# A list scheduler that counts TensorE's instruction blocks, and chunk loads moved behind Gram loads

## The chip, the cores and the metric

The kernel runs on one core of a Trainium2 chip. What counts is the device time of one execution in microseconds (us), from the first to the last instruction with what lies around them; runs of the same kernel are compared by their median.

## The reference

Three layers follow each other. The first is a delta-rule attention with 4 batches, 8 heads, 768 tokens and a head dimension of 48:

```
k_n = k / (norm(k) + 1e-6)
for t in range(S):
    y[t] = q[t] @ state
    v_old = state applied to k_n[t]
    state = state + beta[t] * outer(k_n[t], v[t] - v_old)
```

Its output, 3072 tokens by 384, goes through a soft mixture of experts (logits x @ phi, a softmax over the tokens to make 32 slots, eight experts with 1024 hidden units and a ReLU, a softmax over the slots to combine), and then through a feed-forward layer with 2048 hidden units and g = h * sigmoid(1.702 h). All of it is float32.

## The kernel before

The 768 tokens are cut into 24 chunks of 32 (NS, C). All 32 heads are worked on at once. The work has a *planned* part and a *plain* part.

The planned part is the attention, the logits and the dispatch. For each chunk i there are Gram matrices: load_g brings k and q of the chunk (kq), copy_k copies k, gram runs the matmuls for K with K ("G") and for Q with K ("P") into a PSUM bank, and gram_out copies them out. Four chunks are a group. For each group, solve inverts the triangular systems on VectorE by 31 pairs of steps (lines 517 and 521), between a transpose of the Gram matrices in and one of the result out (both line 477). Chunk i then runs as a chain: V (minus v into PSUM), KS (old state times k), a copy to rbd, U (the inverse times that), a copy to ubd, S (the new state), a copy to sbd; beside it QS and Y give the output. The next chunk needs sbd. load_c brings a chunk's own data (kc, v, k, qc) to the tile cs, which has three buffers; scale_v scales v on GpSimd with the solve's norms (nr). logits transposes the output and multiplies by phi.

Every such step is a call of Plan.add with its engine, an estimated duration, the keys that it reads and writes, and, for TensorE, the columns that it streams. Nothing is sent to an engine yet. Plan.issue then makes a list schedule: listed takes, step by step, for each engine the ready operation with the best rank, and gives it a start time; issue repeats this for several weights and alternates it with backward passes, and keeps the schedule with the shortest length. The operations of each engine, SP's DMA issues among them, are sent in the order of these start times. So the estimates decide the order; on the chip, semaphores decide the times.

Plan.fill goes through the planned TensorE operations: where the gap to the next is over FILL[0] + 2 TURN = 0.54 us and fewer than NEED = 4500 columns lie in the last WIN = 3.4 us of the plan, it puts in dummy matmuls (filler, line 356), to keep TensorE at work. 18 more (PRE) stand at the start.

A float32 matmul call gives two weight loads and two matmuls on TensorE, a transpose one of each.

The plain part follows: the experts and the feed-forward layer, in the order in which they are written down. The diff doesn't touch it.

Before the change the loads of chunks 0 and 1 are added to the plan with i = 0 and i = 1, without a dependency:

```python
        if i < VB - 1:
            load_c(i)
```

Of the kernel before, what the change touches and what calls it, by code (L numbers as in the profile page):

```python
# [19 lines left out]
B, H, S, D = 4, 8, 768, 48  # L20
C = 32
NS = S // C
GS = 4
# [5 lines left out]
VB, UB, XB, XTB, LB = 3, 2, 5, 4, 1  # L29
# [4 lines left out]
NA, NBS = 4, 4  # L34
# [23 lines left out]
class Plan:  # L58
# [10 lines left out]
    WAITS = (4.0, 8.0, 20.0)  # L69
    ROUNDS = 24  # L70

    WIN, NEED = 3.4, 4500
    FILL = (0.24, 384)

    def __init__(self, tc, filler=None):
        self.tc = tc
        self.filler = filler
        self.ops = []
        self.names = []
        self.kinds = []  # L80
        self.wr, self.rd, self.first = {}, {}, {}
        self.beside = {}

    def add(self, eng, dur, fn, reads=(), writes=(), after=0.0, nm="", cols=0, deps=(), beside=None):
        self.names.append(nm)
        k = len(self.ops)
        if eng == "pe":
            dur *= self.PACE
        self.kinds.append(self.KINDS.get(nm.split(".")[0], "rows") if eng == "pe" else eng)
        deps = set(deps)  # L90
        for r in reads:
            if r in self.wr:
                deps.add(self.wr[r])
            self.rd.setdefault(r, []).append(k)
        for w in writes:
            if w in self.wr:
                deps.add(self.wr[w])
            deps.update(self.rd.get(w, ()))
        for w in writes:
            self.wr[w] = k  # L100
            self.rd[w] = []
        deps.discard(k)
        if beside is not None:
            self.beside[k] = beside
            deps.add(beside)
        self.ops.append((eng, dur, fn, deps, after, cols))
        return k
# [7 lines left out]
    def issue(self):  # L115
        ops = self.ops
        n = len(ops)
        pred = [[(d, self.lat(d, k)) for d in ops[k][3]] for k in range(n)]
        succ = [[] for _ in range(n)]
        for k in range(n):  # L120
            for d, l in pred[k]:
                succ[d].append((k, l))
        tail = [0.0] * n
        for k in range(n - 1, -1, -1):
            tail[k] = ops[k][1] + max([tail[q] + l for q, l in succ[k]], default=0.0)
        best = None
        for w in self.WAITS:
            rank = [-t for t in tail]
            for _ in range(self.ROUNDS):
                start = self.listed(rank, pred, succ, w)  # L130
                if best is None or self.length(start) < best[0] - 1e-6:
                    best = (self.length(start), start)
                back = self.listed([-(start[k] + ops[k][1]) for k in range(n)], succ, pred, w)
                end = max(back[k] + ops[k][1] for k in range(n))
                rank = [end - back[k] - ops[k][1] for k in range(n)]
        self.makespan, start = best
        order = sorted((round(start[k], 6), k, k) for k in range(n))
        self.order = order
        idle = self.fill(order) if self.filler else {}
        self.fillers = sum(idle.values())  # L140
        for _, _, k in order:
            for _ in range(idle.get(k, 0)):
                self.filler(self.names[k])
            ops[k][2]()
# [1 line left out]
    def length(self, start):  # L146
        return max(start[k] + o[1] for k, o in enumerate(self.ops) if o[0] not in ("sp", "aq") and o[0][0] != "v")

    def listed(self, rank, pred, succ, wait):


        ops, kinds = self.ops, self.kinds
        n = len(ops)
        left, ready, start = [len(p) for p in pred], [0.0] * n, [0.0] * n
        free, cand, best, last = {}, {}, {}, None
        for k in range(n):
            free.setdefault(ops[k][0], 0.0)
            cand.setdefault(ops[k][0], set())
            if not left[k]:
                cand[ops[k][0]].add(k)  # L160
        stale = set(cand)
        for _ in range(n):
            for e in stale:
                best[e] = None
                for k in cand[e]:
                    t = max(free[e] + (self.TURN if e == "pe" and last not in (None, kinds[k]) else 0.0), ready[k])
                    b = (rank[k] + wait * t, t, k)
                    if best[e] is None or b < best[e]:
                        best[e] = b
            stale.clear()  # L170
            t, e, k = min((b[1], e, b[2]) for e, b in best.items() if b)
            cand[e].discard(k)
            start[k] = t
            t += ops[k][1]
            free[e] = t
            stale.add(e)
            if e == "pe":
                last = kinds[k]
            if e == "pool" and k not in self.beside:
                free["dve"] = max(free["dve"], start[k]) + self.HELD  # L180
                stale.add("dve")
            for q, l in succ[k]:
                left[q] -= 1
                ready[q] = max(ready[q], t + l)
                if not left[q]:
                    cand[ops[q][0]].add(q)
                    stale.add(ops[q][0])
        return start
# [34 lines left out]
def delta_moe_kernel(ctx, tc, kq, vt, kt, bu, phi, w1, w2, win, wout, out):  # L223
    nc = tc.nc
    P = 128
# [84 lines left out]
    kqd = [t_[:, 0:2048].rearrange("p (z h u t) -> p z h u t", z=2, h=2, u=16) for t_ in slots[0:NA]]  # L310
# [65 lines left out]
    def cost(eng, n):  # L376
        return {"dve": (n + 62) / 960.0, "act": 0.052 + n / 1200.0, "pool": 0.15 + 0.00166 * n, "padd": 0.15 + 0.0021 * n}[eng]

    def dma(dst, src, key, d=0.73):
        pl.add("sp", d, lambda: nc.sync.dma_start(dst, src), (), key if isinstance(key, list) else [key], after=2.0)  # L380

    def load_g(i):
        a = i % NA
        for h in range(2):
            dma(kqd[a][64 * h : 64 * h + 48, :, h], kq[i, 64 * h : 64 * h + 48], [("kqd", a, h)] + [("kqd", a, h, z) for z in range(2) if i < 2 * NA], 0.75)
        if i < KCOPY:
            copy_k(i)
        else:
            dma(kds[a][0:112], kq[i, :, 0], [("kd", a, 0), ("kd", a, 1)], 0.85)
# [411 lines left out]
    for i in range(NS):  # L801
        if i == 0:
            load_first()
            for z in range(2):
                for n in range(GS):

                    gram(n, z, [pl.wr["bank", GS - 1]] if z else ())
                if z == 0:
                    pl.wr["bank", GS - 1] = len(pl.ops) - 1
                for n in range(GS):  # L810
                    gram_out(n, z)
            clear_blocks()
        elif GS <= i < 3 * GS:
            grams(i)
        if i < LEAD:
            solves(i)
        if i == 1:
            setup_loads()
        if i < VB - 1:
            load_c(i)  # L820
    clear_banks()
    for i in range(NS):
        n = i + VB - 1
# [317 lines left out]
```

## Time and profile before

| | |
|---|---|
| median of 3 runs | 513.24 us (511.08 to 516.22) |
| profiled execution | 516.4 us |
| its span, first to last instruction | 514.7 us |
| TensorE busy | 470.0 us, 91% of the span |
| VectorE busy | 310.4 us, 60% |
| ScalarE busy | 280.2 us, 54% |
| GpSimd busy | 72.9 us, 14% |
| mean granted TensorE clock, share of full speed | 0.954 |

Durations below come from the profiled execution. Its span leaves out 1.7 us around the instructions. PE is TensorE's matmul, PEld its weight load, DVE VectorE, ACT ScalarE, POOL GpSimd, SP the engine that issues DMAs.

### The profile page before, as it was taken

Reading aid. Unit: us, or ns where it says so; the run is one execution under the profiler, and the core shown is the slowest. Engines: PE = TensorE matmul, PEld = TensorE weight load, DVE = VectorE, ACT = ScalarE, POOL = GpSimd, SP = SyncE. Lnnn points to the kernel's source line nnn. Section 1 sums busy time; section 2 is a strip of 40 time slices with the busy share of each in tenths; the row PEclk is TensorE's granted clock in tenths of the full one; section 3 lists DMA queues with packets and bytes.
Section 4 is the critical chain, followed back from the end, with each engine's and each line's share of the span. In section 5 each row is a group of like instructions: output and inputs, shape, how many; then the busy total and the mean of one; then the engine's idle time right before and its main releaser. Section 6 shows DMA issues by size and latency. Waiting matters only on the chain.

```text
span 514.7 us, 17917 instructions
## 1 busy us (share of the span) xinstructions
PE 470.0 (91%) x7684; PEld 394.7 (77%) x7684; DVE 310.4 (60%) x836; ACT 280.2 (54%) x621; POOL 72.9 (14%) x113
## 2 busy tenths in 40 slices
PE   8789996888987779878999899999999999999997
PEld 8667765556764555645665799999999999999997
DVE  4969998698999999440453998332323323333322
ACT  8353574756684766555342765545454545545452
POOL 5001101021032111400411655000000000000000
PEclk9687999989998997869999999999999999999999
DMA  8787778886357897997599540100100100100101
GB/s 172 185 205 185 190 215 243 222 246 186 108 154 235 272 312 211 300 391 297 183 422 383 175 163 2 62 0 1 62 1 0 63 1 0 62 0 23 39 3 61
DMA packets 35071, 77.65 MB, mean 151 GB/s; under 512 B 4208, under 2 KB 15728, under 8 KB 33840
## 3 DMA queue, kind: packets, MB, share of 16 engines
q1 hardware_dynamic: 34992, 76.51, 47.7%
q8 instruction: 60, 0.98, 0.8%
q14 instruction: 19, 0.16, 0.1%
HBM read 71.39 MB, written 5.11 MB: 149 GB/s over the span
## 4 chain that ended last, share of the span: by engine, by line
PE 78%; issue 8%; ACT 7%; DVE 3%; DMA 3%; SPq 1%; ACTq 0%; DVEq 0%
PE ps_s L1085 13%; PE ps_y L1085 7%; PE ps_g L1085 7%; PE ps_t L1085 6%; PE ps_s L582 4%; PE ps_y L563 4%; PE ps_x L554 3%; PE ps_x L548 3%; ACT sbd L593 3%; PE ps_t L356 3%; PE ps_x L571 3%; DMA wa<-in_kq_dram 3%; PE ps_x L1044 2%; PE ps_s L952 2%; PE ps_g L445 2%
## 5 line engine op out<-in xcount | busy, mean ns | idle before, releaser
L1049 DVE TENSOR_TENSOR glo<-wa,ghi 128x512 fp32r<-128x512 f32 x96 | 71.4, 744 | 127.1 <-ACT wa L1048 127.0
L1085 PE MATMUL ps_s<-wo,ghi 128*128 128x384 f32 x300 | 81.2, 335 | 0.0
L1047 ACT ACTIVATE ghi<-ps_x 128x512 fp32r<-128x512 f32 x64 | 38.4, 600 | 64.5 <-PE ps_x L1044 63.7
L521 DVE TENSOR_TENSOR wb<-wb,wb 128x87 f32<-128x87 f32 (+23 forms) x211 | 67.6, 338 | 1.2
L517 DVE TENSOR_TENSOR wb<-wb,wb 128x87 f32<-128x87 f32 (+24 forms) x211 | 63.4, 317 | 1.3
L593 ACT COPY sbd<-ps_s 64x384 f32<-64x384 f32 x92 | 43.6, 474 | 24.5 <-PE ps_s L582 19.3
L1085 PEld LDWEIGHTS ps_s<-wo,ghi 128*128 128x128 f32 x300 | 54.8, 188 | 1.9
L1085 PE MATMUL ps_g<-wo,ghi 128*128 128x384 f32 x150 | 50.3, 335 | 0.0
L1085 PE MATMUL ps_y<-wo,ghi 128*128 128x384 f32 x150 | 50.3, 335 | 0.0
L700 POOL TENSOR_TENSOR cs<-cs,nr 128x384 f32<-128x384 f32 x24 | 21.8, 916 | 134.3 <-DVE nr L509 39.4
L1085 PE MATMUL ps_s<-wo,glo 128*128 128x384 f32 x150 | 40.6, 335 | 0.0
L1085 PE MATMUL ps_t<-wo,ghi 128*128 128x384 f32 x120 | 40.2, 335 | 0.0
L1048 ACT ACTIVATE wa<-ps_x 128x512 f32<-128x512 f32 x64 | 38.0, 594 | 0.0
L1047 ACT ACTIVATE ghi<-ps_y 128x512 fp32r<-128x512 f32 x32 | 19.2, 600 | 33.0 <-PE ps_y L1044 32.7
L554 PE MATMUL ps_x<-sbd,cs 112*32 112x96 f32 x736 | 27.8, 270 | 10.1 <-issue 7.2
L558 ACT COPY rbd<-ps_x 128x384 f32<-128x384 f32 x48 | 23.0, 488 | 22.9 <-PE ps_x L554 17.3
L554 PEld LDWEIGHTS ps_x<-sbd,cs 112*32 112x32 f32 x736 | 18.1, 119 | 17.3 <-issue 9.9
L356 PE MATMUL ps_t<-warm 128*128 128x96 f32 x142 | 28.0, 342 | 1.1 <-DVE zeros L317 1.1
L575 ACT COPY ubd<-ps_x 128x384 f32<-128x384 f32 x48 | 20.9, 483 | 14.8 <-PE ps_x L571 14.7
L1085 PEld LDWEIGHTS ps_y<-wo,ghi 128*128 128x128 f32 x150 | 28.1, 188 | 0.8
L1085 PEld LDWEIGHTS ps_g<-wo,ghi 128*128 128x128 f32 x150 | 28.2, 188 | 0.7
L563 PE MATMUL ps_y<-sbd,cs 112*32 112x96 f32 x736 | 26.0, 273 | 2.8 <-ACT x L603 1.5
(289 smaller groups left out, 970.0 us busy)
## 6 DMA issues: line engine op xcount, KB each, us to landing
cs<-in_kq_dram SPq DMA_DIRECT2D x48, 224.0 KB, 4.3
wa<-in_kq_dram SPq DMA_DIRECT2D x42, 192.0 KB, 4.3
wb<-in_w_dram SPq DMA_DIRECT2D x16, 384.0 KB, 6.9
wb<-in_w_dram SPq DMA_DIRECT2D x4, 1536.0 KB, 13.4
cs<-in_vt_dram SPq DMA_DIRECT2D x24, 192.0 KB, 3.9
wa<-in_w_dram SPq DMA_DIRECT2D x3, 1536.0 KB, 10.6
out_dram<-wa SPq DMA_DIRECT2D x24, 192.0 KB, 1.9
cs<-in_kt_dram SPq DMA_DIRECT2D x23, 192.0 KB, 3.6
```

What stands on the lines that cost most here:

```text
L356: nc.tensor.matmul(ps[bank][:, 416:512], warm, warm[:, 0:96], start=True, stop=True)
L517: engs[e].tensor_tensor(tmp, xx[:, lo:top, j : j + 1].to_broadcast([P, n, m]), gu[:, j : j + 1, j + 1 :].to_broadcast([P, n, m]), op=ALU.mult)
L521: engs[e].tensor_tensor(xx[:, lo:top, j + 1 :], xx[:, lo:top, j + 1 :], tmp, op=ALU.add)
L554: nc.tensor.matmul(px[g][32 * j : 32 * j + 32, c % 2, :, j % 2], kci[0:112, 4 * j + c], sbd[0:112, j, c].rearrange("p h e -> p (h e)"), st ...
L558: pl.add(re_[g], cost(re_[g], 384), lambda g=g: copy[re_[g]](rbd[:, 2 * g : 2 * g + 2].rearrange("p c h q e -> p (c h q e)"), ps[f"x{g}"][ ...
L563: nc.tensor.matmul(py[c // 2][32 * j : 32 * j + 32, c % 2].rearrange("p h e -> p (h e)"), qci[0:112, 4 * j + c], sbd[0:112, j, c].rearrang ...
L593: apart(sbs, e, copy[e](sbn[r, :, 2 * z : 2 * z + 2, h], ps_s[z][r]))
L700: t = nc.gpsimd.tensor_tensor(v_, v_, nr[:, 8 * st : 8 * st + 8].unsqueeze(2).to_broadcast([P, 8, D]), op=ALU.mult)
L1047: nc.scalar.activation(ghis[k % 3], phs[k % 3], AF.Gelu_apprx_sigmoid)
L1048: nc.scalar.activation(ggs[k % 3], phs[k % 3], AF.Gelu_apprx_sigmoid)
L1049: nc.vector.tensor_tensor(glos[k % 3], ggs[k % 3], ghis[k % 3], op=ALU.subtract)
L1085: nc.tensor.matmul(po[f][:, 0:DM], l_[:, 128 * f : 128 * f + 128], w_out(fc, r), start=(fc == 0 and l_ is ghi and r == 0), stop=False)
```

## The change

The planner gets a table of how many matmul calls an operation has (CALLS), and in its forward passes a count: when 64 (BLOCK) calls are full, the next block starts at the earliest 4.0 us (FETCH) after the block before, and TensorE's free time moves on accordingly. The count begins at 34 (AHEAD). Backward passes don't count. The operation's start time stays; its end moves. The loads of chunks 0 and 1 are added with chunk 7 and depend, in the plan, on the last Gram load of that chunk. Both stand on the same queue, so no semaphore comes with it.

```diff
+    CALLS = {"V0": 4, "V1": 4, "KS0": 4, "KS1": 4, "QS0": 4, "QS1": 4, "U0": 16, "S0": 8, "S1": 8, "Y": 16, "G": 4, "P": 3.5, "T": 1, "L": 8, "D": 4}
+    FETCH, BLOCK, AHEAD = 4.0, 64, 34
...
+        self.calls.append(self.CALLS.get(nm.split(".")[0], 1) + (1 if cols == 664 else 0))
...
-                start = self.listed(rank, pred, succ, w)
+                start = self.listed(rank, pred, succ, w, True)
...
-    def listed(self, rank, pred, succ, wait):
+    def listed(self, rank, pred, succ, wait, forward=False):
...
+        calls, block = self.AHEAD, 0.0
...
+            if e == "pe":
+                last = kinds[k]
+                calls += self.calls[k]
+                if forward and calls >= self.BLOCK:
+                    calls -= self.BLOCK
+                    part = ops[k][1] * min(1.0, calls / max(self.calls[k], 1))
+                    at = max(t - part, block + self.FETCH)
+                    t, block = at + part, at
             free[e] = t
             stale.add(e)
-            if e == "pe":
-                last = kinds[k]
...
+    ahead = []
+
     def dma(dst, src, key, d=0.73):
-        pl.add("sp", d, lambda: nc.sync.dma_start(dst, src), (), key if isinstance(key, list) else [key], after=2.0)
+        return pl.add("sp", d, lambda: nc.sync.dma_start(dst, src), (), key if isinstance(key, list) else [key], after=2.0, deps=list(ahead))
...
-            dma(kqd[a][64 * h : 64 * h + 48, :, h], kq[i, 64 * h : 64 * h + 48], [("kqd", a, h)] + [("kqd", a, h, z) for z in range(2) if i < 2 * NA], 0.75)
+            pl.first["kq", i] = dma(kqd[a][64 * h : 64 * h + 48, :, h], kq[i, 64 * h : 64 * h + 48], [("kqd", a, h)] + [("kqd", a, h, z) for z in range(2) if i < 2 * NA], 0.75)
...
-        if i < VB - 1:
-            load_c(i)
+        if i == 2 * GS - 1:
+            ahead.append(pl.first["kq", i])
+            for n in range(VB - 1):
+                load_c(n)
+            ahead.clear()
```

## Rows read from the trace of the kernel before

**Rows 1.** Busy time by stretch: us, busy (instructions) by engine, granted clock, DMA share, GB/s.

```profile
55.00:157.00 102.00, 86.51 (x3035) 64.20 (x3027) 92.11 (x296) 69.81 (x176) 16.40 (x20) 0.97 0.70 199
157.00:245.00 88.00, 70.57 (x2012) 47.45 (x2012) 60.66 (x178) 52.02 (x134) 14.04 (x35) 0.86 0.85 285
245.00:515.00 270.00, 263.44 (x1789) 242.56 (x1779) 114.51 (x180) 131.50 (x259) 32.84 (x31) 1.00 0.21 81
```

**Rows 2.** The page: TensorE's busy time and instructions; instruction queue: packets, MB, share.

```profile
PE 470.0 (91%) x7684; PEld 394.7 (77%) x7684; DVE 310.4 (60%) x836; ACT 280.2 (54%) x621; POOL 72.9 (14%) x113
...
q8 instruction: 60, 0.98, 0.8%
```

**Rows 3.** Busy time by stretch, between long issue waits, and one dense stretch.

```profile
80.00:89.33 9.33, 7.20 (x254) 5.47 (x254) 7.81 (x24) 5.94 (x14) 0.62 (x2) 1.00 0.82 253
...
159.30:175.57 16.27, 12.52 (x381) 8.32 (x381) 16.27 (x63) 9.86 (x27) 2.81 (x3) 0.90 0.75 233
...
131.00:147.50 16.50, 15.60 (x553) 11.20 (x537) 16.17 (x62) 12.33 (x33) 2.49 (x3) 1.00 0.43 134
```

**Rows 4.** TensorE's waits, 55 to 245 us: us, times, longest (first, last of seven).

```profile
PE ps_x L554 <- issue: 7.2, 5, 2.0
...
PE ps_x L548 <- issue: 0.4, 1, 0.4
```

**Rows 5.** Timeline of TensorE; in brackets, idle before and its releaser.

```profile
108.52 0.38 PE L445 MATMUL ps_g<-wa 112*32 112x64 f32 x10 [2.54 <-issue]
```

**Rows 6.** Timeline of VectorE: transposes of the solves.

```profile
33.08 1.97 DVE L477 STREAM_TRANSPOSE wb<-gs 128x1024 f32<-128x1024 f32 x1 [4.08 <-ACT gs L463]
...
50.27 2.00 DVE L477 STREAM_TRANSPOSE gs<-wb 128x1024 f32<-128x1024 f32 x1
57.98 2.00 DVE L477 STREAM_TRANSPOSE wb<-wb 128x1024 f32<-128x1024 f32 x1
...
114.02 2.18 DVE L477 STREAM_TRANSPOSE wb<-wb 128x1024 f32<-128x1024 f32 x1
...
204.10 2.00 DVE L477 STREAM_TRANSPOSE gs<-wb 128x1024 f32<-128x1024 f32 x1
```

**Rows 7.** Timeline of TensorE: first Gram parts, fillers, V and U of some chunks.

```profile
13.20 0.65 PE L445 MATMUL ps_g<-wa 112*32 112x64 f32 x32 [0.79 <-DMA wa<-in_kq_dram]
...
16.87 0.53 PE L445 MATMUL ps_x<-wa 112*32 112x64 f32 x19 [2.27 <-issue]
...
49.04 5.38 PE L356 MATMUL ps_t<-warm 128*128 128x96 f32 x46
54.35 0.86 PE L548 MATMUL ps_x<-cs,negi 128*32 128x192 f32 x16
...
55.53 0.89 PE L571 MATMUL ps_x<-rbd,gs 64*32 64x96 f32 x32
...
119.73 0.73 PE L571 MATMUL ps_x<-rbd,wb 64*32 64x96 f32 x26
...
216.00 0.56 PE L571 MATMUL ps_x<-rbd,gs 64*32 64x96 f32 x32
```

**Rows 8.** Timeline of SP's DMA issues at the start.

```profile
7.04 0.34 SPq L380 DMA_DIRECT2D cs<-in_kq_dram  x1
13.95 8.07 SPq L380 DMA_DIRECT2D wa<-in_kq_dram  x8
22.07 0.57 SPq L380 DMA_DIRECT2D cs<-in_kq_dram  x1
```

**Rows 9.** Busy time by stretch, where the moved loads would lie.

```profile
22.00:31.00 9.00, 9.00 (x218) 7.31 (x217) 7.01 (x35) 3.93 (x8) 0.00 (x0) 0.66 0.97 230
```

**Rows 10.** Timeline of ScalarE: the last Gram copy of the third group.

```profile
49.44 0.38 ACT L468 COPY wb<-ps_y 128x256 f32<-128x256 f32 x1
```

**Rows 11.** Fillers alone (line 356), by stretch: PE and PEld busy, clock, DMA.

```profile
55.00:157.00 102.00, 0.46 (x2) 0.30 (x2) 0.97 0.70 199
157.00:245.00 88.00, 0.46 (x2) 0.30 (x2) 0.86 0.85 285
```

More of the change, by code (lines that the diff above doesn't have):

```diff
@@ L79, in __init__ @@
         self.names = []
-        self.kinds = []
+        self.kinds, self.calls = [], []
         self.wr, self.rd, self.first = {}, {}, {}
```

## Prediction

> **What bounds the kernel now.** I read the busy time by stage first [rows 1]. The last 270 us, from 245 us on, are the experts and the second feed-forward layer; there TensorE is busy 263.4 us. The planner does not order that part, so the change can only move the 245 us ahead of it. In those, no engine is full: from 55 to 157 us TensorE is busy 86.5 of 102 us and VectorE 92.1, from 157 to 245 us TensorE 70.6 of 88 and VectorE 60.7, at a granted clock of 0.86 against 0.97 in the stretch before.
>
> Next I asked how TensorE gets its instructions. Queue 8 moved 60 packets, 0.98 MB in all, so 16 KB a packet; TensorE ran 7684 matmuls and as many weight loads [rows 2]. That is 256 instructions, or 128 matmul-and-load pairs, to a packet, which I call a block. Then I counted pairs between long waits that the profile puts down to "issue", that is to nothing it sees [rows 3]: 254 from one such wait to the second after it, 381 over a third stretch. These are 2 and 3 times 127, a block less a few semaphore instructions. So these waits fall at block borders, once a block is used up and the next is not there.
>
> The price of a border has two forms. As a rate: 131 to 147.5 us holds 553 pairs [rows 3], 4.32 blocks at 3.82 us each, with TensorE busy 15.6 of 16.5 us. All of 55 to 157 us holds 3035 pairs, 23.7 blocks at 4.30 us; 157 to 245 us holds 2012, 15.7 blocks at 5.60 us [rows 1]. The first stretch is within 13% of the quickest rate seen, the second is not near it. As waits: TensorE's list of waits has seven lines released by "issue" from 55 to 245 us, 23.5 us in all [rows 4]; one of 2.54 us stands in the middle of a Gram matrix [rows 5]. That list is the most that spacing can give back.
>
> **The change part by part.** Nothing that computes is added or removed. The planner's cost of TensorE gains a rule: 64 calls (each fp32 call is two pairs, so 64 are a block) may not start less than 4.0 us after the 64 before. The load order changes, and with both the order on every engine. I take four terms against the profiled execution, 516.4 us.
>
> (a) *The start.* VectorE runs the first triangular solve, then stops 4.08 us until 33.08 us for the second group's Gram copies [rows 6], with the rest of solve 0 queued behind that transpose. The planner thought those copies earlier. One reason it could not know is TensorE's border wait of 2.27 us before 16.87 us, in the Gram matrices that hold the buffers of the next loads [rows 7]. If the planner counts it, the transpose moves behind more of solve 0 and VectorE fills the hole. Bounds: nothing, and the whole 4.08 us. I take 2 us, by the 2.27 us row. It reaches the end only if chunk 0 follows: its first matmul stands at 54.35 us behind 46 records of fillers from 49.04 us, and its U at 55.53 us though solve 0's matrix is turned by 52.27 us [rows 6, 7]. Fillers are placed by the same plan, so I let the whole front move: -2.
>
> (b) *The loads.* Four of the eight loads of chunks 0 and 1 left SP by 7.04 us, ahead of the eight second-group Gram loads that start at 13.95 us; the others stood behind those already, from 22.07 us [rows 8]. So only four are moved, some 0.8 MB. What the Gram loads gain is small, for they wait on TensorE's reading of their buffers, not on SP; the one wait for data here is TensorE's 0.79 us before 13.20 us [rows 7]. On the other side, the 0.8 MB now lie in 22 to 31 us, where the DMA engines are 97% busy at 230 GB/s [rows 9]: 3.5 us more of queue, ahead of the third group's Gram loads. What hides it: the copies of that group end at 49.82 us [rows 10] and VectorE takes them at 57.98 us [rows 6], 8.2 us later; chunk 0's own data is not read before 47 us. On SP the four pass the eight Gram loads and nothing else; POOL's queue loses nothing, for its first scaling of v waits for the solve, not for the load. I take 0, bounds -0.8 and, if that cover is gone, +3.5.
>
> (c) *The borders.* Bound of the gain: all 23.5 us of waits; the first stretch at 3.82 us a block would be 90.6 us, so 11.4 of them could go there. Bound of the loss: a worse order can cool TensorE; if the first stretch had the clock of the second, its 86.5 us busy would become 97.6, +11. Nearer to the truth is a fraction of the gain. A border's wait goes only if TensorE would have waited for another engine at that moment, or if less urgent work stands there. VectorE stands against most of it in the first stretch: solve 2's matrix is turned at 116.2 us and chunk 8's U starts at 119.73 us, 3.5 us later [rows 6, 7], so TensorE may gain no more than that before VectorE is late. At the end there is room: the last solve is done at 206.1 us, the U that needs it starts at 216.00 us [rows 6, 7]. I take a quarter of 23.5: -6.
>
> (d) *Fillers.* These dummy matmuls go wherever the plan shows TensorE idle by over 0.54 us and few columns in the window before. The stalls that the planner now models look idle to that rule. From 55 to 245 us there are now four filler records, two fillers [rows 11]. The 46 records before chunk 0, 23 fillers, took 5.38 us [rows 7], 0.23 us each. With a filler at one border in six of the 39, 6 to 7 fillers, that is +1.5. Bounds: 0, and one or two at each border, 9 to 18 us, if none hides in the wait.
>
> Sum: -2 + 0 - 6 + 1.5 = -6.5, so 509.9 us for an execution like the profiled one. That one lies 3.2 us above the median of the runs; taken from the median 513.24, it is 506.7, and I say 507.
>
> [...] The longest border wait here is 2.54 us [rows 5]. [...]
>
> **The rivals.**
> *Rate, not waits* (0.27): between 55 and 157 us blocks and VectorE both fill the time, so an order that moves waits only moves them; what one chunk saves the next spends. For it: 4.30 against 3.82 us a block, VectorE busy 92.1 of 102. Against: 10 us slack at the last solve. Then (a) -2, (c) at most -1.5, (d) +1.5: 511 to 513, say 512.
>
> *Fillers in the modelled stalls* (0.15, the side of slower): the stall is at the border, the fillers stand after it in TensorE's stream, so the engine first waits for its block and then runs them. Two at each of 39 borders are 78, 17.9 us with 78 calls or 1.2 more blocks, 4.7 us; less (a) and (c), 8: +14, if all lie on the path, half of it if half do: 520 to 527. It decides from 35 fillers in 55 to 245 us (8 us at 0.23); above that the change loses.
>
> *The count drifts* (0.10): the plan counts no fillers of the fill rule and takes 3.5 calls for a Gram part that issues three from chunk 4 on. The 23 fillers before chunk 0 [rows 7] alone are a third of a block. Then the modelled borders lie in other instructions than the chip's, the change doesn't do what it says, and the order is just another order: 513, give or take 6.
>
> *Borders cost nothing* (0.03): the issue waits have another cause in the stream and stay whatever the spacing, so (c) is 0: 513.24 - 2 + 1.5, again 513. Against it stand the multiples of 127 [rows 3]. [...]
>
> **How the numbers follow.** My forecast, 507, has 0.45; its own range is 499 to 512: 513.2 - 4.1 - 12 + 1.5 with the whole hole and half of the waits gone, 513.2 - 3 + 1.5 with no hole filled and an eighth of them gone. The range for 8 in 10 reaches up into the rivals: 498 to 521. Within 1%, about what a measurement of this kernel can tell from no change, is 508.1 to 518.4. Faster by more: 0.38 of my case, 0.06 of rate, 0.03 of drift, 0.47 together. Slower by more: 0.13 of fillers, 0.03 of drift and 0.02 of the rest, 0.18. Same: 0.35.
>
> **What would show it.** (a): the hole before the second Gram transpose on VectorE under 2.5 us and chunk 0's first U before 54 us. (b): four more loads of chunk data behind the Gram loads on SP, and no wait for them on POOL or TensorE. (c): the issue lines of TensorE from chunk 0 on sum to under 18 us, and us per block in the later stretch falls from 5.60. (d): filler records in the chunk stage between 4 and 30. The stage from 245 us on must keep its 270 us. I'm wrong if the issue waits shrink while the waits for ScalarE's copies grow by as much, if the granted clock of the second stretch drops below 0.86, or if fillers pass 70 records.

## The result and the profile after

The change makes the kernel slower by a little. In runs side by side on one chip the kernel before took 517.19 us (median of 21, two of them far off at 711 and 1435 us) and the changed one 519.82 us (median of 21, 515.92 to 524.45); the ratio is 1.0073, 95% interval 1.0048 to 1.0097. Run again beside other kernels it gave 1.0063 (1.0036 to 1.009). In some executions a kernel takes over 1.5% longer than in its fastest; the ratios leave these out, and a * in the table of experiments stands where the profiled execution was such a one. The forecast was 507, 6.2 us below the 513.24 that it started from; the kernel before itself took 4 us more here than in its first three runs.

| profiled execution | before | after |
|---|---|---|
| time / span | 516.4 / 514.7 us | 519.82 / 518.1 us |
| mean granted clock | 0.954 | 0.957 |
| chunk 0's V starts, last Y ends | 54.35, 245.1 us | 55.55, 247.6 us |
| issue waits of TensorE between the two | 23.5 us | 27.7 us |
| from the last Y to the plain part's first matmul | 7.5 us | 8.5 us |
| plain part | 262.1 us | 262.0 us |

The last rows of the table already hold the answer in outline: the plain part is the same, and all of the 3.4 us by which the span is longer lie in the planned part. Of them, 2.5 are there when the last Y ends. The other 1.0 comes behind it: the new order leaves more of the logits work (one transpose and one product with phi more) behind the last Y. The plain part starts here, first before, then after:

```profile
252.62 1.50 PE L920 MATMUL ps_x<-wa,sit 128*32 128x256 f32 x24
256.10 1.50 PE L936 MATMUL ps_x<-wa,sit 128*32 128x256 f32 x24
```

This is the page of the changed kernel, as in [rows 2]. The work is the same: ten matmul records more, which are fillers.

```profile
PE 470.5 (91%) x7694; PEld 395.2 (76%) x7694; DVE 314.6 (61%) x836; ACT 280.3 (54%) x621; POOL 73.6 (14%) x113
...
q8 instruction: 60, 0.98, 0.8%
```

Busy time by stretch, in the columns of [rows 1] (length, then busy time and count of PE, PEld, DVE, ACT, POOL, then granted clock, DMA share, GB/s):

```profile
0.00:55.00 55.00, 48.85 (x858) 40.35 (x859) 41.31 (x184) 26.79 (x53) 9.15 (x27) 0.84 0.73 170
55.00:157.00 102.00, 86.51 (x2915) 63.35 (x2916) 91.87 (x294) 67.78 (x170) 17.51 (x19) 0.95 0.72 203
157.00:245.00 88.00, 68.02 (x2065) 46.57 (x2066) 66.96 (x180) 52.59 (x135) 14.10 (x37) 0.90 0.88 283
248.00:518.00 270.00, 264.09 (x1784) 242.86 (x1783) 114.51 (x180) 131.54 (x259) 32.82 (x31) 1.00 0.21 81
```

Between 55 and 157 us TensorE is busy for the same 86.51 us as in [rows 1], but did 120 records fewer (2915 for 3035). At 128 records a block that is 4.48 us a block, for 4.30 before. In the later stretch it is 5.45 for 5.60. So the plan did not make the early blocks quicker, and the late ones hardly.

Then TensorE's list of waits from 55 to 248 us, the lines released by "issue", for comparison with [rows 4] (us in total, times, longest):

```profile
PE ps_s L595 <- issue: 8.0, 5, 4.4
PE ps_x L567 <- issue: 5.5, 5, 2.0
PE ps_y L612 <- issue: 4.6, 4, 2.1
PE ps_y L576 <- issue: 4.1, 3, 1.7
...
PE ps_x L561 <- issue: 1.9, 1, 1.9
PE ps_x L584 <- issue: 1.4, 2, 0.7
...
PE ps_g L458 <- issue: 1.2, 1, 1.2
PE ps_t L627 <- issue: 0.6, 1, 0.6
PE ps_t L638 <- issue: 0.4, 1, 0.4
```

They add up to 27.7 us with the small ones and have moved to other lines (the largest sum was KS, line 554, before; it is S, line 595, now), but have not shrunk. The longest is 4.4 us, for 2.54 before [rows 5], and it lies on the chain from chunk to chunk. The timeline of TensorE shows it in the second half (S1) of chunk 7's state update; the first rows are the start of chunk 0:

```profile
48.90 6.71 PE L367 MATMUL ps_t<-warm 128*128 128x96 f32 x58
55.55 0.86 PE L561 MATMUL ps_x<-cs,negi 128*32 128x192 f32 x16
56.34 0.69 PE L367 MATMUL ps_t<-warm 128*128 128x96 f32 x4
56.95 0.67 PE L584 MATMUL ps_x<-rbd,gs 64*32 64x96 f32 x32
...
115.55 0.71 PE L595 MATMUL ps_s<-ubd,cs 64*48 64x96 f32 x24
120.70 0.57 PE L595 MATMUL ps_s<-ubd,cs 64*48 64x96 f32 x8 [4.44 <-issue]
...
127.82 0.56 PE L584 MATMUL ps_x<-rbd,wb 64*32 64x96 f32 x32
```

A block ends after 24 of the 32 matmuls. What follows waits for the last 8: the copy to sbd, then KS, and so chunk 8's U at 127.82 us, 16.0 us after chunk 7's at 111.83. Before, these two U were 7.2 us apart, and the widest gap between any two was 11.1. The busy time of the two stretches from that wait on shows what came with it:

```profile
115.90:120.70 4.80, 0.36 (x20) 0.22 (x9) 4.11 (x12) 0.35 (x2) 0.00 (x0) 0.92 0.50 111
120.70:127.80 7.10, 7.10 (x179) 6.01 (x178) 0.00 (x0) 4.46 (x12) 1.56 (x2) 0.57 0.48 146
```

TensorE hardly works for 4.8 us, and then runs at a granted clock of 0.57, with 179 records in 7.1 us. The clock was 1.00 from 115.9 to 119.9 us, 0.50 from 121 to 126 and 1.00 again from 126.9 us on. VectorE does nothing in the second of the two.

At the start the timeline above has 62 records of fillers around chunk 0's V (58 and 4) where before had 48, 46 of them in [rows 7]; chunk 0's U is at 56.95 us, 1.4 later than before in this execution. VectorE's hole before the second Gram transpose, 4.08 us in [rows 6], is now 5.78:

```profile
35.05 1.96 DVE L490 STREAM_TRANSPOSE wb<-gs 128x1024 f32<-128x1024 f32 x1 [5.78 <-ACT gs L476]
```

The issues of SP, against [rows 8]:

```profile
5.15 0.43 SPq L393 DMA_DIRECT2D cs<-in_vt_dram  x1
5.62 0.43 SPq L393 DMA_DIRECT2D cs<-in_kq_dram  x1
6.10 0.63 SPq L393 DMA_DIRECT2D cs<-in_kt_dram  x1
14.35 8.52 SPq L393 DMA_DIRECT2D wa<-in_kq_dram  x8
22.92 0.58 SPq L393 DMA_DIRECT2D cs<-in_vt_dram  x1
```

Three chunk loads still stand ahead of the eight Gram loads. They are chunk 2's: the third buffer of cs is free too, the change gave no dependency to its loads, and they slipped into the place that those of chunks 0 and 1 left.

### The profile page after: what moved, and what is told of

The parts are those of the page before. It is cut to its first block, busy times and chain, and to the rows that moved or that the text cites. A ratio compares the mean times of both kernels' runs of the same rounds, so it can differ in the third digit from the quotient of the medians.

```text
span 518.1 us, 17928 instructions
## 1 busy us (share of the span) xinstructions
PE 470.5 (91%) x7694; PEld 395.2 (76%) x7694; DVE 314.6 (61%) x836; ACT 280.3 (54%) x621; POOL 73.6 (14%) x113
## 4 chain that ended last, share of the span: by engine, by line
PE 76%; issue 9%; ACT 7%; DMA 4%; DVE 3%; SPq 1%; ACTq 0%; DVEq 0%
PE ps_s L1101 13%; PE ps_y L1101 6%; PE ps_g L1101 6%; PE ps_t L1101 6%; PE ps_s L595 4%; PE ps_y L576 4%; DMA wa<-in_kq_dram 4%; ACT sbd L606 3%; PE ps_x L567 3%; PE ps_x L561 3%; PE ps_t L367 3%; PE ps_x L584 3%; PE ps_x L1060 2%; PE ps_t L627 2%; PE ps_s L968 2%
## 5 line engine op out<-in xcount | busy, mean ns | idle before, releaser
L534 DVE TENSOR_TENSOR wb<-wb,wb 128x31 f32<-128x31 f32 (+25 forms) x211 | 66.5, 335 | 2.0
L530 DVE TENSOR_TENSOR wb<-wb,wb 128x135 f32<-128x135 f32 (+25 forms) x211 | 65.4, 328 | 2.0
L567 PE MATMUL ps_x<-sbd,cs 112*32 112x96 f32 x736 | 29.8, 279 | 8.1 <-issue 5.5
L1063 ACT ACTIVATE ghi<-ps_y 128x512 fp32r<-128x512 f32 x32 | 19.2, 600 | 33.0 <-PE ps_y L1060 33.0
L595 PE MATMUL ps_s<-ubd,cs 64*48 64x96 f32 x736 | 23.3, 257 | 11.4 <-issue 8.0
L571 ACT COPY rbd<-ps_x 128x384 f32<-128x384 f32 x48 | 23.2, 490 | 18.5 <-PE ps_x L567 11.5
L576 PE MATMUL ps_y<-sbd,cs 112*32 112x96 f32 x736 | 25.7, 259 | 5.5 <-issue 4.1
L595 PEld LDWEIGHTS ps_s<-ubd,cs 64*48 64x48 f32 x736 | 17.0, 122 | 17.8 <-issue 10.7
## 6 DMA issues: line engine op xcount, KB each, us to landing
wa<-in_kq_dram SPq DMA_DIRECT2D x42, 192.0 KB, 4.4
cs<-in_vt_dram SPq DMA_DIRECT2D x24, 192.0 KB, 4.4
out_dram<-wa SPq DMA_DIRECT2D x24, 192.0 KB, 1.9
cs<-in_kt_dram SPq DMA_DIRECT2D x23, 192.0 KB, 4.7
```

The costliest lines, as they stand in the source:

```text
L530: engs[e].tensor_tensor(tmp, xx[:, lo:top, j : j + 1].to_broadcast([P, n, m]), gu[:, j : j + 1, j + 1 :].to_broadcast([P, n, m]), op=ALU.mult)
L534: engs[e].tensor_tensor(xx[:, lo:top, j + 1 :], xx[:, lo:top, j + 1 :], tmp, op=ALU.add)
L567: nc.tensor.matmul(px[g][32 * j : 32 * j + 32, c % 2, :, j % 2], kci[0:112, 4 * j + c], sbd[0:112, j, c].rearrange("p h e -> p (h e)"), st ...
L571: pl.add(re_[g], cost(re_[g], 384), lambda g=g: copy[re_[g]](rbd[:, 2 * g : 2 * g + 2].rearrange("p c h q e -> p (c h q e)"), ps[f"x{g}"][ ...
L576: nc.tensor.matmul(py[c // 2][32 * j : 32 * j + 32, c % 2].rearrange("p h e -> p (h e)"), qci[0:112, 4 * j + c], sbd[0:112, j, c].rearrang ...
L595: nc.tensor.matmul(ps_s[z][64 * h : 64 * h + 48, j].rearrange("p c e -> p (c e)"), ki[64 * z : 64 * z + 64, j, h], ubd[64 * z : 64 * z + 6 ...
```

## The experiments

Two theories stood against each other. *Misplaced count*: the plan's borders lie elsewhere than the chip's, so the spacing protects the wrong instructions. Followed through TensorE's stream, the changed plan's borders are 28 to 32 calls away from the chip's from chunk 0 to chunk 11, which is half a block and so as far off as can be, some 25 to chunk 15 and 20 to 10 behind that; the 28 fillers ahead of chunk 0, which the plan doesn't count, are the main reason. *Conserved waits*: TensorE meets its next block late at nearly every border wherever that falls, so an order can move a wait but not remove it, and one order is as good as another but for luck. A third was that the moved loads cost something.

All ratios are against the kernel before on the same chip, in five rounds. The last two columns are from one profiled execution: issue waits of TensorE from chunk 0's V to the last Y, and the time from chunk 7's U to chunk 8's.

| run | ratio | 95% interval | issue waits, us | U7 to U8, us |
|---|---|---|---|---|
| before | 1 | | 23.5 | 7.2 |
| changed kernel | 1.0073 | 1.0048 to 1.0097 | 27.7 | 16.0 |
| e9_after_again | 1.0063 | 1.0036 to 1.009 | 26.9 | 15.3 |
| e1_count_only | 1.0029 | 0.999 to 1.0067 | 24.1 | 15.5 |
| e10_count_again | 1.0043 | 1.0005 to 1.0081 | 25.6 | 14.8 |
| e2_loads_only | 0.9898 | 0.9808 to 0.9989 | * | * |
| e12_loads_again | 1.002 | 0.9988 to 1.0051 | * | * |
| e3_count_aligned | 0.9972 | 0.993 to 1.0014 | 27.3 | 7.4 |
| e4_phase45 | 0.9958 | 0.9921 to 0.9995 | 28.1 | 8.9 |
| e13_after_half_block | 1.0287 | 1.021 to 1.0364 | 30.8 | 10.4 |
| e14_before_half_block | 1.0231 | 1.0173 to 1.0288 | 23.1 | 8.8 |
| e17_after_half_block_2 | 1.0096 | 1.005 to 1.0142 | 28.6 | 9.5 |
| e18_before_half_block_2 | 1.0114 | 1.0067 to 1.0161 | 25.4 | 8.5 |
| e5_before_quarter | 0.9825 | 0.978 to 0.987 | 20.3 | 8.9 |
| e6_aligned_quarter | 0.9736 | 0.9693 to 0.978 | 19.2 | 8.0 |
| e7_cap_fillers | 0.9973 | 0.9947 to 1.0 | 26.2 | 9.3 |
| e8_other_draw | 1.0038 | 1.0001 to 1.0074 | 29.1 | 12.2 |
| e11_fetch5_aligned | 1.0279 | 1.022 to 1.0338 | 21.5 | 20.3 |
| e15_aligned_cap | 0.9989 | 0.9938 to 1.004 | * | * |
| e16_aligned_cap_loads | 1.0065 | 1.003 to 1.0101 | 25.7 | 7.5 |

### The two parts alone

The count with the loads back at their old place, in e1_count_only and once more in e10_count_again; the changed kernel itself once more, in e9_after_again:

```diff
-        if i == 2 * GS - 1:
-            ahead.append(pl.first["kq", i])
-            for n in range(VB - 1):
-                load_c(n)
-            ahead.clear()
+        if i < VB - 1:
+            load_c(i)
```

The loads moved with the count off, in e2_loads_only and e12_loads_again:

```diff
-                start = self.listed(rank, pred, succ, w, True)
+                start = self.listed(rank, pred, succ, w)
```

> The block count stays, the loads of chunks 0 and 1 go back to their old place in the plan; the order on TensorE, VectorE, ScalarE and GpSimd is then that of the changed kernel, and only SP's differs. Theory A (the counted blocks make the order worse, since the modelled borders lie half a block from the chip's): as the changed kernel, 1.004 to 1.010 times before, issue waits of TensorE from chunk 0 on 25 us or more. Theory B (the moved loads cost the time, by a later start): 0.997 to 1.003 times before.

> The loads are moved, no block is counted; the order on all engines but SP is that of the kernel before. Theory A: within 0.3% of before, issue waits near 23.5 us. Theory B: 1.004 to 1.010 times before, with the second transpose of the solves (33.08 us before, 35.05 us after) late by 2 us.

> The changed kernel once more, beside its two parts on one chip. Its first ratio was 1.0073 (1.0048 to 1.0097): 1.004 to 1.010 again.

> The block count alone, once more (first ratio 1.0029, 0.999 to 1.0067). If the order of the counted plan carries the loss, it agrees with the changed kernel within 0.3%; if the moved loads carry part of it, it is at least 0.3% below the changed kernel.

> The moved loads alone, once more (the first comparison was too uncertain: 0.981 to 0.999). If the load order alone does nothing: 0.997 to 1.003. If it costs: 1.003 to 1.008.

The count alone is 0.3 to 0.4% slower (no change is just inside the first run's interval, just outside the second's), and it has the border in chunk 7's state update too, with waits of 3.02 and 1.71 us where the changed kernel has 4.44. The six runs of e2_loads_only scatter from 510.13 to 520.99 us, and their median, 518.28, is close to the 517.59 of the kernel before beside them, so the 0.9898 isn't used; repeated, it is 1.002. In the plan the four computing engines have the very same order with the loads moved as without, with the count on or off: the move is one of SP's order alone. The loads may cost 0.2 to 0.3%, or nothing; the last pair of runs below points the other way.

### The count brought into line

```diff
-        self.calls.append(self.CALLS.get(nm.split(".")[0], 1) + (1 if cols == 664 else 0))
+        self.calls.append(self.CALLS.get(nm.split(".")[0], 1) + (1 if cols == 664 else 0) + (30 if nm == "V0.0" else 0))
```

In e4_phase45 the 30 is 45.

> As the changed kernel, but V0 of chunk 0 counts 30 calls more in the plan, for the fillers that stand ahead of it; the modelled borders then lie within 5 calls of the chip's up to chunk 16 (30 off in the changed kernel). Theory A: the issue waits fall under 20 us and the time to 0.985 to 0.997 times before. Theory C (the place of the borders doesn't matter: the order is another draw, and the waits come whatever the plan thinks): anywhere from 0.99 to 1.01, issue waits 22 to 29 us.

> As before, but 45 calls more instead of 30: the modelled borders lie some 20 calls from the chip's on the other side. Theory A: between the changed kernel and the aligned one, 1.000 to 1.007 times before, issue waits 22 to 27 us. Theory C: anywhere from 0.99 to 1.01, with no order between this, the aligned and the changed kernel.

With 30 the plan's borders lie within 5 calls of the chip's up to chunk 15; with 45 they are some 20 off. Both are about 1% faster than the changed kernel, their intervals apart from its, and not measurably faster than before (the second by 0.4%, at the edge of its interval). But the waits didn't shrink: 27.3 and 28.1 us. And the kernel that is 20 calls off is no worse than the one in line. So the count in line does not do what it was to do; that the gain over the changed kernel is just that of a different order fits, but is not shown.

### The same order with the borders moved

These move the chip's borders by half a block and leave the order on every engine as it is, with 32 more dummy calls at the very start. In the changed kernel that puts the chip's borders within 7 calls of the plan's up to chunk 15, and takes the one out of chunk 7's state update. The kernel before has the same shift as a control.

```diff
-    def filler(bank=FBANK):
-        nc.tensor.matmul(ps[bank][:, 416:512], warm, warm[:, 0:96], start=True, stop=True)
+    def filler(bank=FBANK, m=P, n=96):
+        nc.tensor.matmul(ps[bank][:m, 416 : 416 + n], warm[:, 0:m], warm[:, 0:n], start=True, stop=True)
...
-    for _ in range(PRE):
-        filler()
+    for n in range(PRE + 32):
+        filler(FBANK, *((P, 96) if n < 11 else (32, 64)))
```

This is e17_after_half_block_2 and e18_before_half_block_2. In e13_after_half_block and e14_before_half_block 12 dummies kept 96 columns and 38 had 8, with all 128 columns of weights.

> The changed kernel with the same order of work on every engine; only the dummy matmuls at the very start are different: 50 calls (12 of 96 columns, 38 of 8) in place of 18 of 96, so 32 calls more, half a block. With that every later block border on the chip falls half a block earlier in TensorE's stream, which is where the plan has it in chunks 0 to 16 (in the changed kernel the plan was 28 to 32 calls off there), and no border falls where chunk 7's second state update now waits 4.44 us. If the offset of half a block is why the change lost: the issue waits from 55 us on fall from 27 us to under 18, chunk 7 to chunk 8 takes 10 us and not 16, and the time is 508 to 512. If waits are conserved, because TensorE meets each border before its block is there: issue waits stay at 24 to 29 us, chunk 7 gets its time back (some 3 us of the 6), and the time is 515 to 518, no better than before.

> The kernel before with the same shift by 32 dummy calls at the start; its order knows nothing of borders. It prices where the borders happen to fall, alone: within 0.5% of before (514.5 to 520) if a place of the borders is a small draw, issue waits 22 to 29 us from 55 us on. If half a block in itself were worth 1% or more, this one would show it too, in either direction.

> The changed kernel, same order on every engine, with the chip's borders moved half a block earlier as in the run with 38 narrow dummies, but without that run's late start: there the 100 records at the start took 18.39 us, 0.18 us each however few columns, and the first Gram matmul stood at 19.43 us in place of 8.25. Here 11 dummies stay and 39 have 32 columns of weights, like the Gram parts, which ran at some 0.03 us a record; the start should take 7 to 9 us. If the offset of half a block is why the change lost: issue waits from 55 us on under 18 us, time 508 to 512. If waits are conserved: 25 to 29 us (28.0 in the run with the late start), chunk 7 to chunk 8 about 10 us in place of 16.0, time 514 to 518, no better than before by more than 0.5%.

> The kernel before with the same start, so the same shift by half a block in an order that knows nothing of borders: within 0.5% of before, issue waits 22 to 27 us from 55 us on. It prices the place of the borders alone, and the new start.

The first pair failed as a test: a dummy record of 8 columns took 0.10 us at a granted clock of 1.00, one of 96 columns 0.12 [rows 7], the granted clock fell to 0.51 while TensorE ran them, and the first Gram matmul came at 19.43 us instead of 8.25. TensorE's timeline of e13_after_half_block (all 50 dummies are one row, named by its first), and its busy time with dummies of 8 columns alone, ahead of the fall and behind it (PE, PEld, clock, DMA share, GB/s):

```profile
1.11 18.39 PE L367 MATMUL ps_t<-warm 128*128 128x96 f32 x100 [1.11 <-DVE zeros L328]
19.43 0.66 PE L458 MATMUL ps_g<-wa 112*32 112x64 f32 x16
...
5.90:8.30 2.40, 2.40 (x24) 2.40 (x24) 1.00 0.81 159
8.30:19.40 11.10, 11.10 (x55) 11.10 (x54) 0.51 0.61 122
```

The second pair starts 1.9 us late. In e17_after_half_block_2 chunk 7's update is whole:

```profile
1.11 9.30 PE L367 MATMUL ps_t<-warm 128*128 128x96 f32 x99 [1.11 <-DVE zeros L328]
10.20 0.26 PE L458 MATMUL ps_g<-wa 112*32 112x64 f32 x3
...
120.42 0.88 PE L595 MATMUL ps_s<-ubd,cs 64*48 64x96 f32 x32
```

Chunk 7 to chunk 8 then takes 9.5 us, where it took 16.0. That is what the border there had cost, and it went. The waits did not shrink with it: from chunk 0's V to the last Y it is 196.6 us (192.0 in the changed kernel, 194.2 in the control), and the issue waits are 28.6 us (30.8 in the first pair, counted to the last Y), in the very order that the plan made, with the borders near where it had put them. The control is 1.1% slower than before; its later start, some 1.9 us, is 0.4% of that. Beside it the changed order is no longer slower (1.0096 and 1.0114, 0.2% faster with 0.7% of noise either way); in the first pair it still is, by 0.5% with 1% of noise. So these pairs show that the waits stay. Whether the loss of 0.7% goes with the border they leave open.

### Fewer bytes for the fetch to compete with

The first-layer weights of the experts, most of which load beside chunks 16 to 23, take a quarter of their rows: three quarters of this load are left out, and the experts compute with stale values, so this is no faster kernel but a probe. The plan's costs and order stay.

```diff
-            k = pl.add("sp", 1.3, lambda dst=dst, src=src, lo=lo: nc.sync.dma_start(dst[:, lo : lo + PIECE], src[:, lo : lo + PIECE]), (), wr, after=2.0, deps=[pl.first[mark, i]], nm=nm)
+            k = pl.add("sp", 1.3, lambda dst=dst, src=src, lo=lo, r=96 if nm[:2] == "w1" else 0: nc.sync.dma_start(dst[r:, lo : lo + PIECE], src[r:, lo : lo + PIECE]), (), wr, after=2.0, deps=[pl.first[mark, i]], nm=nm)
```

A few clears of unused buffers on GpSimd at the start go with it. It was done to the kernel before and to the one with 30 calls added.

> The kernel before, its plan unchanged, but the 24 prefetched pieces of w1 load only 32 of their 128 rows (the rest of the weights is left out, so the experts compute with stale values): 7 MB less DMA, most of it from 157 us on. Theory R (a border's wait comes from the block fetch, which starts late when the DMA engines are loaded): the issue waits of TensorE from 157 to 245 us fall from 10.9 to under 6 us, a block there from 5.60 to under 5.2 us, the time to 0.975 to 0.990 times before. Theory N (the waits have to do with the order alone): waits and time within 0.5% of before.

> The aligned block count with the same pieces of w1 cut to 32 rows. If the spacing of 4.0 us is right once the fetch is prompt, this plan now gains over the uncounted one: at least 0.5% below the kernel before with cut pieces, with fewer issue waits than there. If a plan cannot move these waits at all, the two agree within 0.4%.

The busy time from 157 to 235 us, first of the kernel before:

```profile
157.00:235.00 78.00, 61.44 (x1761) 41.42 (x1764) 60.66 (x178) 46.26 (x120) 14.04 (x35) 0.85 0.88 289
```

and of e5_before_quarter, whose last Y ends at 235.0 us:

```profile
157.00:235.00 78.00, 64.67 (x2014) 43.40 (x2014) 60.59 (x179) 52.09 (x134) 15.88 (x35) 0.93 0.73 232
```

Its list of TensorE's waits there:

```profile
PE ps_y L607 <- issue: 4.1, 2, 3.7
PE ps_x L562 <- issue: 1.7, 3, 0.8
```

With the DMA engines at 0.73 instead of 0.88 TensorE gets through 253 records, two blocks, more in the same 78 us, in an unchanged plan; the issue waits there are 5.8 us, for 10.5 in the kernel before. The whole kernel gains 1.75%. The clock rose with it, 0.85 to 0.93. The count in line then comes out 0.9% below e5_before_quarter (e6_aligned_quarter, 0.9736 / 0.9825 = 0.991, intervals that touch at 0.978). That the spacing earns this is not shown: the issue waits are 19.2 us for 20.3, a difference of 1.1, while chunk 0's V to the last Y takes 7.4 us less, and there was no other order as a control.

### Fillers and another draw

e7_cap_fillers is the kernel before with at most ten dummies in one gap:

```diff
         idle = self.fill(order) if self.filler else {}
+        idle = {k: min(v, 10) for k, v in idle.items()}
```

e8_other_draw is the kernel before with another value of one planner constant that has nothing to do with borders:

```diff
-    PACE = 1.05
+    PACE = 1.06
```

> The kernel before with at most 10 fillers in one gap, so 10 instead of 22 ahead of chunk 0; all orders stay. If the fillers hold up chunk 0 (54.35 us, where the solve's matrix is turned by 52.27), its first U comes 1.5 to 3 us sooner, and the time is 0.994 to 0.998 times before if the chunks are bound by the chain behind it; within 0.2% if blocks or VectorE give it back.

> The kernel before with PACE 1.06 in place of 1.05: no block is counted, but the list schedule comes out in another order (a quarter of TensorE's operations move). Theory C (any new order is a draw, good or bad by half a per cent, and the border waits come with it): 0.992 to 1.010 times before, issue waits 20 to 30 us. If only the count or the loads could move the time, within 0.2%.

With the cap chunk 0's U came 2.1 us sooner, at 53.4 us, but the last Y at 246.0, 0.9 later in that execution; over the runs it gains 0.3%, with no gain at the edge of its interval. So the early start is spent again on the way, at least in that execution, and as 24 filler records fewer gave 0.3%, the 14 more around chunk 0 in the changed kernel can be no more than a part of its loss. The other draw moves the time by 0.4% (0.01 to 0.74) for no reason of borders, and the waits to 29.1 us.

### A stricter count

```diff
-    FETCH, BLOCK, AHEAD = 4.0, 64, 34
+    FETCH, BLOCK, AHEAD = 5.0, 64, 34
```

This on top of the 30 calls.

> The aligned count with 5.0 us between blocks, near the 5.3 to 5.6 us that a block takes on the chip from 157 us on, where 4.0 is too short. Theory R1 (the count fails because its spacing is too short where the DMA engines are loaded): 0.985 to 0.996 times before and better than the aligned count at 4.0 us (0.9972). Theory R2 (TensorE waits for a block at nearly every border, so its rate is given and no plan moves it): 0.995 to 1.005, issue waits from chunk 0 on 22 to 30 us.

The busy time of e11_fetch5_aligned:

```profile
55.00:157.00 102.00, 83.00 (x2658) 58.58 (x2650) 98.16 (x297) 64.94 (x161) 14.25 (x17) 0.92 0.68 188
```

For comparison, the same stretch of e3_count_aligned, which differs from it in the 5.0 alone:

```profile
55.00:157.00 102.00, 84.92 (x2922) 61.93 (x2921) 98.31 (x314) 68.34 (x173) 14.36 (x17) 0.95 0.71 203
```

The issue waits do fall, from 27.3 to 21.5 us, but the last Y ends at 258.2 us instead of 246.7. TensorE did 264 records less in the stretch, two blocks, with VectorE as busy as before. So it has fewer waits for its blocks because the order asks for fewer blocks in the time: 11.5 us are paid for 5.8 us of waits. The widest gap between two chunks' U is 20.3 us.

### In line, with fewer fillers, and with the loads either way

```diff
+        self.calls.append(self.CALLS.get(nm.split(".")[0], 1) + (1 if cols == 664 else 0) + (20 if nm == "V0.0" else 0))
...
+        idle = {k: min(v, 10) for k, v in idle.items()}
```

e15_aligned_cap is the changed kernel with these two lines (20 calls bring this order within 8 calls up to chunk 16). e16_aligned_cap_loads has the loads of chunks 0 and 1 back as well.

> The changed kernel with the count brought into line (20 calls more at chunk 0's first V) and at most 10 dummy matmuls in one gap. The plan's borders are within 5 calls of the chip's up to chunk 16. If alignment pays: 508 to 512. If waits are conserved: issue waits 24 to 29 us, 514 to 517, with 1 to 2 us of it from fewer dummies ahead of chunk 0 (its U sooner by 2 us, part of which is spent again).

> As the run before it (count in line, at most 10 dummies in a gap), with the loads of chunks 0 and 1 back at their old places; the orders of the four computing engines are the same in both. If the moved loads cost 0.2 to 0.3%, this one is 1 to 1.5 us faster than the other; if SP's order at the start is hidden, the two agree within 1 us.

In line, with at most ten fillers in a gap and no border in chunk 7's update (7.5 us from U to U in the second of the two, which has the same order), it is as fast as before, not faster. That is no clean price of the count in line, for this order loses behind the last Y. In e16_aligned_cap_loads the last Y ends at 243.4 us, 1.7 sooner than in before. But then TensorE runs the next 20 us at a granted clock of 0.74, with 6 filler records behind the last Y where before has 12:

```profile
243.40:263.40 20.00, 19.06 (x181) 12.24 (x178) 6.50 (x25) 6.00 (x19) 6.22 (x11) 0.74 0.74 299
```

In before and in the changed kernel it is 1.00 there. From the last Y to the end it takes 274.8 us for 269.6, 5.2 more. e11_fetch5_aligned has the same 6 records, the same 0.74 and 274.7 us.

With the loads back it is slower by 0.8%, with 0.6% of noise either way, than with them moved, although the computing engines' orders are the same: the opposite of what e1_count_only had shown against the changed kernel. So no cost of the moved loads is shown in either direction, and SP's order alone may move the time by some tenths of a per cent.

## Why the prediction was wrong

**Step (c) failed**, in the sentence "A border's wait goes only if TensorE would have waited for another engine at that moment, or if less urgent work stands there", from which came a quarter of 23.5, -6 us. It took the border as a fixed gap that a plan can fill with something. The runs showed a delivery, at a pace that no order of the work quickened. The 60 packets of queue 8 can be set against TensorE's records one by one: in the trace of before, at 33 of 38 borders from 55 us to the last Y, TensorE goes on 2.2 to 3.1 us after the packet of the next block began to move (34 of 38 in the changed kernel). So it met its block late, or just in time, nearly everywhere. The packet starts after the border before it: some 1.1 us after it on the mean when the DMA engines are under 40% busy, 1.8 at 60 to 80%, 2.8 above 95% (six traces). Together that is 3.7 to 5.4 us a block, and the quickest 3.82 of [rows 3] is the light end of it. A block whose records were done earlier waited, whichever records they were. So term (c) was not -6: the waits it was to shorten by a quarter went from 23.5 to 27.7 us. In every order with full DMA load the waits were 23 to 31 us, in line or not, in the same order with the borders moved, with the count or without. Under that are only e11_fetch5_aligned, which asked for fewer blocks in the time, and the two kernels with fewer bytes.

**The start value.** The sum was taken from the profiled execution (509.9) down to the median of three runs, 3.2 us lower. Side by side, 21 runs put that median at 517.19, above the profiled 516.4. So some 4 of the 12.8 us between 507 and 519.82 are that median's, and the rest is a forecast of 6.2 us less where 2.6 more came. That 519.82 lies within 498 to 521 is owed to the width of that range, not to its mechanisms.

**(a)** forecast -2, from a hole that closes. It did not close: it is 5.78 us here and 4.26 in e9_after_again, the same kernel, for 4.08 before; chunk 0's U came at 56.95 and 55.72 us, for 55.53. One execution of a kernel differs from the next by as much, so that the start got later is not shown, only that nothing was gained. The plan put 14 filler records more ahead of chunk 0 and its U. In the run with the cap a start sooner by 2.1 us was gone at the last Y, so it is doubtful too that this term reaches the end.

**(b)** the term, 0, holds within what could be measured, but not as it was told, so that is luck in part: not four more loads behind the Gram loads but a swap, with chunk 2's three in front. I had read the dependency for the loads that it is given to, and not asked what else was ready for SP.

**(d)** +1.5 from 4 to 30 filler records in the chunk stage; between chunk 0's U and the last Y there are none. The fillers are at chunk 0, 62 records against 48. The rival of fillers in the stalls is dead with that, though the time came out on its side.

**Rivals.** *Rate, not waits* was the nearest in mechanism: moved, not removed. It looked for the rate on VectorE, where it is TensorE's instruction supply (3.7 to 5.4 us a block); and it still gave the start its -2. *The count drifts* named the uncounted fillers and was right that borders were half a block off, the worst place; but with the count in line the waits stay, so that is not why they don't shrink. The 0 of *Borders cost nothing* for (c) is nearer to what the runs show than the -6, though for another reason than its own: the waits do lie at the borders, and with the full load 21.5 us or more of them stayed in every order.

**What the loss of 0.7% is** remains partly open. It comes back (1.0073, 1.0063). In four executions of this order of the computing engines (twice the changed kernel, twice the count alone), a border lies in chunk 7's state update, at a price of 1.7 to 4.4 us of wait and a low clock (0.57) after it in the worst. It is a feature that sets these four apart from the orders in line at 0.9958 to 1.0065. But from chunk 0's V to the plain part's first matmul these four take 198.4 to 201.5 us, and the order of before, without and with the cap, 198.3 and 201.3: no price of that border is left there, and the profiled executions do not place the loss. Taking it away in the same order gave 6.5 us at that place, no time against before, and against the controls no clear answer. Other orders scatter by up to half a per cent, so a draw of the order is a sufficient account; that this border is the cause is not shown.

## What to carry to other kernels

Before spacing work around an engine's instruction blocks, look at when the block's packet starts and lands. Here TensorE met it late, or just in time, at 33 of 38 borders; the order had nothing to give, and time was to be had from the bytes that move beside it (1.75% for three quarters of the weights' load, with the same order). Fewer instructions might be another place, which was not tried here. The model's fixed gap of 4.0 us stood against 3.7 to 5.4 us a block on the chip, and with the count in line 27.3 us of waits were left; the stricter one of 5.0 us held back the work itself, by 264 records from 55 to 157 us. And redraw the order once for no reason first: here that moved the time by 0.4%, so that a change by half a per cent says little of the idea behind it. Last, don't read a change of a start or a hole from one execution: here the same kernel's hole was 5.78 and 4.26 us.

## What the hardware showed that was not expected

The instruction fetch was quicker with less data beside it. With the load of weights cut, from 0.88 to 0.73 of the DMA engines' time, blocks from 157 us to the last Y took 4.86 us on the mean, for 5.49, and the packet started 1.88 us after the border for 2.34.

A dummy matmul with 128 columns of weights took about as long here with 96 columns streamed as with 8. At a granted clock of 1.00, 46 records of 96 columns took 5.38 us, 0.12 each [rows 7], and 24 of 8 columns 2.40 us, 0.10 each; at 0.51, 55 of 8 columns took 11.10 us, 0.20 each. The 18.39 us of that start hold stretches of both clocks. With 32 columns of weights and 64 streamed, the dummies of e17_after_half_block_2 took 0.06 each at 1.00:

```profile
5.50:10.20 4.70, 4.70 (x80) 4.61 (x80) 1.00 1.08 194
```

So the cheapest spacer of the three was the one with few weights.

The border in chunk 7's state update cost more than itself at its place: 4.44 us of wait, then 7.1 us at a granted clock of 0.57, and 16.0 us from U to U for the 9.5 of the same order without it.
